# Pair 1 of a fused recurrence and MoE kernel loaded one token a row on GpSimd's queue, with a new instruction order

## The chip, the cores and the metric

The kernel runs on one core of one Trainium2 chip. A core has TensorE (matrix products, with a separate weight load), VectorE, ScalarE and GpSimd for the elementwise work, SyncE, which only issues transfers, and 16 DMA engines that all issuing engines share. The metric is the device time of one execution in microseconds (us); lower is better. Times within a profile count from the first instruction of the span. All engines run their own instructions strictly in order and wait for each other through semaphores.

## The reference

The kernel computes a gated linear recurrence over 768 tokens for 4 batches and 8 heads of 48 channels, and then feeds its output, as 3072 tokens of 384 channels, through two layers with a GELU between them.

```python
def _attn_ref(q, k, v, alpha):            # each (4, 8, 768, 48)
    state = zeros((B, H, D, D))
    for t in range(S):
        state = alpha[:, :, t, :, None] * state + einsum('bhd,bhe->bhde', k[:, :, t], v[:, :, t])
        y[:, :, t] = einsum('bhd,bhde->bhe', q[:, :, t], state)
    return y

def _moe_ref(x, w_in, w_out):             # x (3072, 384), w_in (384, 2048), w_out (2048, 384)
    h = x @ w_in
    g = 0.5 * h * (1.0 + tanh(sqrt(2 / pi) * (h + 0.044715 * h * h * h)))
    return g @ w_out
```

All inputs and the output are float32.

## The kernel before

**Tiling.** The 768 tokens of a batch are cut into 6 chunks of 128. One batch's chunk is a *unit* (128 tokens on the partitions, 8 heads x 48 channels along the row), two neighbouring batches' units make a *pair*, so there are 12 pairs, 0 to 11; pairs 0 and 1 are chunk 0. Within a chunk the recurrence is done as a masked attention with decay: `ln` takes the log of alpha (ScalarE), `cum` sums it over the tokens with an upper triangular matrix (TensorE), `b`, `binv` and `bend` are exponentials of the sums (ScalarE), `qp` = q*b and `kp` = k*binv (VectorE), `t` turns both so that channels lie on the partitions (TensorE) and `ev` copies them out of PSUM, `attn` multiplies them, `mask` keeps the lower triangle (VectorE), `y` multiplies the masked products with v, `x` copies y to bf16, `tx` turns it and `xe` copies it to `xT`. `kv` and `st` carry the state on to the next chunk. From pair 2 on the state's part of y is computed beside the attention. From pair 6 on the turns of q, k and x are transposing DMAs on SyncE's queue (`turn`).

**The two layers.** Layer 1 (`l1`, L658) makes the hidden tiles of a pair: each task is 6 products of 128 x 256 columns into one PSUM bank, and eight tasks make a pair's block; task `l1m.i` needs quarter i//2 of w_in, `xT` of both units, and one of the four PSUM buffers `ff`. `gelu` (ScalarE) empties it. Layer 2 (`l2`, L677) makes a unit's output in four tasks of four products of 384 columns, each needing one quarter of w_out; `ot` copies it out and `store` writes it.

**Two ways of laying out a pair.** Pairs 0 and 1 are `PACKED` (L179): q, k and alpha come with four tokens of a head in one row (768 bytes in one piece, L341), which needs a special sum (`cum_packed`, L375: 7 products with two block triangular matrices and 4 small ones for the last row), rearranging copies, and a turn back of k (`turn_back`, L511, and its copy L523) before `kv`. Their units are handled one at a time (`SINGLE`, `EARLY`). Pairs 2 and up come with one token a row (192 bytes a piece, one head each). Pairs 2 to 5 are turned as row tiles (`turn_halves`, L474: 32 products of 64 x 64 that go two at a time, copies in two halves, L491), and the last row of the sums is taken by VectorE's 32 x 32 transposes (`last_row`, L586) instead of by `bend`. `SPLIT` pairs are loaded and summed a unit at a time.

**Transfers.** `RINGS` lists the loads on the hardware queues: q, k and alpha of pairs 0 and 1 by unit, twelve loads of 192 KB; numbers in `BY_ACT` are issued by ScalarE, the rest by SyncE. `LOADS` lists what GpSimd's queue issues, in order; a `gate` is a small GpSimd copy that reads a tile and so holds that queue until the tile has landed. v of the `NARROW` pairs 0 and 1 is loaded as float32 and cast by VectorE or ScalarE (`narrow`, L423); all other v are cast by the DMA. The weights are cast by the DMA too.

**The order.** `Scheduler` (L47 to L165) builds the order of all instructions. `FIRST` (L184) is a list written out of every step, `E:task` with E one of P (TensorE), V (VectorE), A (ScalarE), G (GpSimd) and S (SyncE); `order()` puts the tasks in that order. Only the order of the steps of one engine matters for the chip: what is emitted is each engine's queue, and the waits between engines. `fill.n` steps are n idle products on TensorE (L322). `LANDED` holds landing times in nanoseconds that the scheduler assumes for the loads named; the numbers count the loads as they are declared, first those of `RINGS`, then those of `LOADS`.

PSUM has 8 banks: one double buffer `ca` of two banks, two `yk` and four `ff`. `CUM_FF` pairs keep their sums in `ff`, `AT_FF` names the units whose attention products go to `ff`.

The head of the old `FIRST`, by engine, is: SyncE alpha, alpha, q, k of pair 0 and then pair 1's; ScalarE q and k of unit 0 of pair 0; GpSimd gate on pair 0's second alpha, v of pair 0, gate on its second k, w_in 0, v of pair 1, w_in 1, 2, 3, w_out 0, 1, the first halves of pair 2. TensorE has `fill.7`, the packed sums of both units, and then ten more idle products in seven places between the steps of pairs 0 and 1.

Of the kernel before, what the change touches and what calls it, by code (L numbers as in the profile page):

```python
# [7 lines left out]
F32 = mybir.dt.float32  # L8
# [163 lines left out]
class _Kernel:  # L172

    BLOCKS = ((0,), (1,), (2,), (3,), (4,), (5,), (6,), (7,), (8,), (9,), (10,), (11,))
    SPLIT = (2,)
    EARLY = (0, 1)
    LOADS = ('gatea 0 1', 'v0', 'gatek 0 1', 'in 0', 'v1', 'in 1', 'in 2', 'in 3', 'out 0', 'out 1', '2a', 'out 2', '2b', 'out 3', '3', '4', '5', 'win3', '6', '7', '8', '9', '10', '11')

    PACKED, CUM_FF, R = (0, 1), (0, 1), 4  # L179
    RINGS = (('a', 0, 0, 1), ('a', 0, 1, 2), ('q', 0, 0, 1), ('k', 0, 0, 1), ('q', 0, 1, 2), ('k', 0, 1, 2),  # L180
             ('a', 1, 0, 1), ('a', 1, 1, 2), ('q', 1, 0, 1), ('k', 1, 0, 1), ('q', 1, 1, 2), ('k', 1, 1, 2))
    BY_ACT = (2, 3,)

    FIRST = """  # L184
        A:table.0 A:load.2 A:load.3 S:load.0 S:load.1 S:load.4 A:ln0.0 S:load.5 P:fill.7 P:cum0.0 A:ln0.1 G:gate.0 G:load.12 S:load.6 P:cum0.1 A:b0.0
        S:load.7 A:bend0.0 V:qp0.0 A:binv0.0 A:binv0.1 S:load.8 V:kp0.0 P:fill.2 P:t0.0 A:b0.1 V:ev0.0 P:fill.1 P:t0.1 S:load.9 A:ev0.1 V:qp0.1
        S:load.10 A:bend0.1 P:fill.3 P:attn0.0 V:kp0.1 G:gate.1 S:load.11 P:t0.2 G:load.13 V:mask0.0 A:ev0.2 P:t0.3 G:load.14 V:mask0.1 A:ev0.3
        P:fill.1 P:t0.4 V:ev0.4 P:fill.1 P:attn0.1 A:ln1.0 G:load.15 P:t0.5 V:mask0.3 P:cum1.0 A:ev0.5 G:load.16 V:vb0.0 A:ln1.1 P:y0.0 V:mask0.2
        G:load.17 P:kv0.0 A:binv1.0 P:cum1.1 V:st0.0 A:x0.0 G:load.18 A:vb0.1 V:kp1.0 P:tx0.0 A:b1.0 P:y0.1 V:xe0.0 G:load.19 V:qp1.0 P:t1.1 A:x0.1
        A:bend1.0 G:load.20 A:b1.1 P:fill.1 P:t1.0 A:ev1.0 V:ev1.1 G:load.21 V:qp1.1 P:fill.1 P:kv0.1 V:st0.1 G:load.22 A:binv1.1 A:bend1.1 P:tx0.1  # L190
        P:attn1.0 V:xe0.1 G:load.23 G:load.24 G:load.25 G:load.26 P:t1.2 P:l10.0 V:kp1.1 V:mask1.0 V:mask1.1 G:load.27 G:load.28 P:t1.3 A:ev1.2
# [513 lines left out]
    def tasks(self):  # L705
# [59 lines left out]
        for m, (c, i) in enumerate(pairs):  # L765
# [40 lines left out]
            if m in self.SPLIT:  # L806
                cums[1].deps += exps[:2]
# [228 lines left out]
```

## Time and profile before

| what | us |
|---|---|
| median of 3 runs (173.99 to 174.16) | 174.1 |
| the profiled execution | 173.77 |
| its span, first to last instruction | 171.9 |
| TensorE busy | 166.3 |
| layer 1 products (L658, 576) | 69.4 |
| layer 2 products (L677, 416) | 68.9 |
| attention products (L552, 192) | 8.0 |
| idle products (L327, 17) | 6.5 |
| ScalarE busy | 125.5 |
| VectorE busy | 107.7 |
| GpSimd busy | 63.0 |

A busy time counts a product from its issue to its modelled end, and products overlap in the pipeline, so a group's busy time is more than the time that the queue spends on it: six products of layer 1 are 0.65 us of the queue. "Idle before" in the waits is time in which an engine had nothing running, with what ended it. The DMA queues moved 29.4 MB, 17.7 of them on GpSimd's queue. The column PEclk of the page is the clock that the throttle granted; it reads 1.00 in every window.

### The profile page before, as it was taken

To read this page: it belongs to the slowest core of one execution; us is meant where nothing else is said; L and a number is where in the kernel's file an instruction comes from. 1 tells how busy PE (TensorE), PEld (TensorE's weight loads), DVE (VectorE), ACT (ScalarE), POOL (GpSimd) and SP (SyncE) were. 2 spreads that over 40 slices of the span, in tenths; PEclk is the share of its full clock that TensorE was granted. 3 is DMA by queue.
4 is the path that set the end of the run, shared out by engine and by line. 5 is a ranking of instruction groups with operands and counts; after the bars stand their busy time and mean duration, and the time that the engine had idled before them with its cause. 6 is when DMAs were issued, how large, how long until landed. Compare 5 with 4: busy or idle time off the path is not lost.

```text
span 171.9 us, 4595 instructions
## 1 busy us (share of the span) xinstructions
PE 166.3 (97%) x1909; PEld 129.8 (75%) x1909; DVE 107.7 (63%) x210; ACT 125.5 (73%) x205; POOL 63.0 (37%) x88
## 2 busy tenths in 40 slices
PE   7999999999999999999999999999999999999991
PEld 2566899666886896797697797796797978987860
DVE  6499820588978999998892898865947550100100
ACT  4578889897999798899779499868882636651412
POOL 2396546986504674933565435320000000000000
PEclk9999999999999999999999999999999999999999
DMA  4999999999999999999999999897967504001212
GB/s 138 311 268 217 199 247 230 231 230 228 256 208 96 257 218 241 169 165 242 145 224 213 158 226 138 181 233 60 232 186 148 147 1 114 4 0 40 101 48 92
DMA packets 51541, 29.40 MB, mean 171 GB/s; under 512 B 39616, under 2 KB 47936, under 8 KB 51520
## 3 DMA queue, kind: packets, MB, share of 16 engines
q0 software_dynamic: 26464, 17.70, 62.3%
q1 hardware_dynamic: 24512, 11.01, 30.8%
q10 hardware_dynamic: 544, 0.39, 0.8%
q8 instruction: 15, 0.25, 0.6%
q14 instruction: 6, 0.05, 0.1%
HBM read 25.17 MB, written 4.72 MB: 174 GB/s over the span
## 4 chain that ended last, share of the span: by engine, by line
PE 91%; DMA 3%; ACT 3%; DVE 0%; issue 0%; DVEq 0%
PE hT L658 37%; PE acc L677 37%; PE at L552 4%; DMA k<-in_k_dram 3%; PE yps L627 2%; PE cum L416 2%; PE kv L581 2%; PE qkT_ps L484 1%; PE xT_ps L646 1%; PE qkT_ps L470 1%; PE yps L561 1%; ACT qkT L508 1%; PE k_ps L516 1%; ACT L318 1%; PE idle L327 1%; PE yps L617 1%
## 5 line engine op out<-in xcount | busy, mean ns | idle before, releaser
L658 PE MATMUL hT<-xT,w_in 128*128 128x256 bf16 x576 | 69.4, 273 | 0.0
L677 PE MATMUL acc<-w_out,gT 128*128 128x384 bf16 (+3 forms) x416 | 68.9, 314 | 0.0
L664 ACT ACTIVATE gT<-hT 128x512 bf16<-128x512 f32 x96 | 53.6, 600 | 15.2 <-PE hT L658 13.1
L658 PEld LDWEIGHTS <-w_in 128*128 128x128 bf16 x576 | 60.6, 114 | 1.2 <-DMA w_in<-in_moe_w_in_dram 0.3
L677 PEld LDWEIGHTS <-gT 128*128 128x128 bf16 x416 | 37.4, 98 | 20.2
L571 DVE TENSOR_TENSOR atm<-at,ut 128x512 bf16<-128x512 f32 x48 | 30.1, 683 | 8.2 <-PE at L552 8.0
L689 DVE COPY ot<-acc 128x384 f32<-128x384 f32 (+2 forms) x9 | 4.3, 488 | 20.0 <-PE acc L677 20.0
L689 ACT COPY ot<-acc 128x384 f32<-128x384 f32 (+1 forms) x17 | 7.9, 472 | 11.6 <-PE acc L677 9.3
L595 DVE STREAM_TRANSPOSE tr<-b 32x256 f32<-32x256 f32 x32 | 14.0, 438 | 1.4 <-ACT b L449 0.8
L346 POOL DMA_DIRECT2D k<-in_k_dram x11 | 12.2, 1111 | 5.7 <-DMA v<-in_v_dram 1.7
L346 POOL DMA_DIRECT2D a<-in_alpha_dram x11 | 12.3, 1117 | 4.4 <-issue 1.7
L460 DVE TENSOR_TENSOR qp<-q,b 128x768 bf16<-128x768 f32 (+1 forms) x15 | 11.9, 792 | 2.8 <-ACT b L449 2.6
L346 POOL DMA_DIRECT2D vb<-in_v_dram x11 | 12.2, 1105 | 3.6 <-issue 1.9
L346 POOL DMA_DIRECT2D q<-in_q_dram x11 | 12.2, 1112 | 2.5 <-DMA w_out<-in_moe_w_out_dram 1.0
L449 ACT ACTIVATE binv<-cum 128x768 bf16<-128x768 f32 (+1 forms) x15 | 10.1, 684 | 3.3 <-PE cum L416 3.3
L460 DVE TENSOR_TENSOR kp<-k,binv 128x768 bf16<-128x768 f32 (+1 forms) x15 | 11.9, 791 | 0.5 <-ACT binv L449 0.5
L318 ACT ACT_TABLE_LOAD x9 | 11.5, 1283 | 0.9 <-PEq L1020 0.7
L449 ACT ACTIVATE b<-cum 128x768 f32<-128x768 f32 (+1 forms) x15 | 10.3, 685 | 2.0 <-PE cum L416 1.5
L664 ACT ACT_TABLE_LOAD x9 | 11.5, 1283 | 0.2
L606 DVE TENSOR_TENSOR stmp<-kv,st 128x384 f32<-128x384 f32 x16 | 8.9, 555 | 1.9 <-PE kv L581 1.2
L608 DVE TENSOR_TENSOR st<-stmp,tr 128x384 bf16<-128x384 f32 x16 | 8.9, 558 | 0.6
L399 ACT ACTIVATE la<-a 128x768 f16<-128x768 f32 (+1 forms) x11 | 8.5, 784 | 0.1
(74 smaller groups left out, 144.8 us busy)
## 6 DMA issues: line engine op xcount, KB each, us to landing
out_dram<-ot SPq DMA_DIRECT2D x19, 192.0 KB, 3.0
a<-in_alpha_dram POOLq DMA_DIRECT2D x9, 384.0 KB, 7.8
q<-in_q_dram POOLq DMA_DIRECT2D x9, 384.0 KB, 8.8
k<-in_k_dram POOLq DMA_DIRECT2D x9, 384.0 KB, 6.9
vb<-in_v_dram POOLq DMA_DIRECT2D x9, 192.0 KB, 6.3
w_in<-in_moe_w_in_dram POOLq DMA_DIRECT2D x4, 384.0 KB, 8.9
w_out<-in_moe_w_out_dram POOLq DMA_DIRECT2D x4, 384.0 KB, 11.0
out_dram<-ot SPq DMA_DIRECT2D x9, 96.0 KB, 1.9
```

Of the source, the lines that this page charges most:

```text
L318: nc.scalar.add_instruction(mybir.InstLoadActFuncSet(name=nc.get_next_instruction_name(), act_func_set_id=i, engine=mybir.EngineType.Activ ...
L346: dma(u[t][:, lo:hi].rearrange("t b h d -> t (b h) d"), src.rearrange("b h s d -> s (b h) d")[c * C:(c + 1) * C])
L449: self.nc.scalar.activation(u[n].rearrange("t i h d -> t i (h d)")[:, lo:hi], cum, AF.Exp, scale=1.0 if n == "b" else -1.0)
L460: self.nc.vector.tensor_tensor(out, rows, b, op=ALU.mult)
L571: self.nc.vector.tensor_tensor(u["atm", i][:, o], u["at", i][o], self.ut[:, None, :].to_broadcast([self.C, self.H // 2, self.C]), op=ALU.mult)
L595: self.nc.vector.transpose(u["tr"][f:f + 32, :, 0:32], rows[:, lo:lo + H * 2 * D].rearrange("t (g n) -> t g n", n=2 * D)[:, :, 0:32])
L606: nc.vector.tensor_tensor(s, acc, old, op=ALU.add)
L608: nc.vector.tensor_tensor(new, acc, end[:, :, None].to_broadcast([C, H // 2, 2 * D]), op=ALU.mult)
L658: self.nc.tensor.matmul(h[:, s].rearrange("p (g t) -> p g t", t=self.C), w_in[:, j, nt % 4 + s], self.xT[c % self.NX][:, lo:hi, j], start= ...
L664: return lambda e: self.nc.scalar.activation(self.gT[c % self.NG][:, nt:nt + 2, lo * self.C:hi * self.C], f.pop(("h", c, lo, nt)), AF.Gelu ...
L677: self.nc.tensor.matmul(f["acc", c, b][:, lo:hi], self.gT[c % self.NG][:, nt, b * self.C:(b + 1) * self.C], self.w_out[:, nt, lo:hi], star ...
L689: self.copy(e)(f["ot", c, b][:, sl], f["acc", c, b] if half is None else f["acc", c, b, half][:, sl])
```

## The change

The changed kernel treats pair 1 like pair 2 (split, one token a row, row tiles, last row by VectorE), but without a state. Its q, k and alpha leave the hardware queues and become half loads on GpSimd's queue, between w_in 0 and w_in 1. v of pairs 0 and 1 is cast by the DMA, v of pair 1 in two halves. GpSimd's first gate is on the first alpha instead of the second, and the gate on k is gone. ScalarE issues one load instead of two. Pair 1's sums stay in `ff`, now one bank for each unit. Four of pair 0's layer-1 tasks (`APART`) are split by unit: `h1` does unit 0, `l1` unit 1 of the same bank. Layer 2 no longer names all layer-1 tasks of pairs 0 and 1 as a dependency. `FIRST` is new from the first step to the last; it keeps `fill.7` and has no other idle products.

```diff
-    SPLIT = (2,)
-    EARLY = (0, 1)
-    LOADS = ('gatea 0 1', 'v0', 'gatek 0 1', 'in 0', 'v1', 'in 1', 'in 2', 'in 3', 'out 0', 'out 1', '2a', 'out 2', '2b', 'out 3', '3', '4', '5', 'win3', '6', '7', '8', '9', '10', '11')
+    SPLIT = (1, 2)
+    EARLY = (0,)
+    LOADS = ('gatea 0 0', 'v0', 'in 0', 'a1', 'q1', 'k1', 'in 1', 'v1', 'in 2', 'in 3', 'out 0', 'out 1', '2a', 'out 2', '2b', 'out 3', '3', '4', '5', 'win3', '6', '7', '8', '9', '10', '11')
-    PACKED, CUM_FF, R = (0, 1), (0, 1), 4
-    RINGS = (('a', 0, 0, 1), ('a', 0, 1, 2), ('q', 0, 0, 1), ('k', 0, 0, 1), ('q', 0, 1, 2), ('k', 0, 1, 2),
-             ('a', 1, 0, 1), ('a', 1, 1, 2), ('q', 1, 0, 1), ('k', 1, 0, 1), ('q', 1, 1, 2), ('k', 1, 1, 2))
-    BY_ACT = (2, 3,)
+    PACKED, CUM_FF, R = (0,), (0, 1), 4
+    RINGS = (('a', 0, 0, 1), ('a', 0, 1, 2), ('q', 0, 0, 1), ('k', 0, 0, 1), ('k', 0, 1, 2), ('q', 0, 1, 2))
+    BY_ACT = (2,)
     FIRST = """
-        A:table.0 A:load.2 A:load.3 S:load.0 S:load.1 S:load.4 A:ln0.0 S:load.5 P:fill.7 P:cum0.0 A:ln0.1 G:gate.0 G:load.12 S:load.6 P:cum0.1 A:b0.0
-        S:load.7 A:bend0.0 V:qp0.0 A:binv0.0 A:binv0.1 S:load.8 V:kp0.0 P:fill.2 P:t0.0 A:b0.1 V:ev0.0 P:fill.1 P:t0.1 S:load.9 A:ev0.1 V:qp0.1
-        S:load.10 A:bend0.1 P:fill.3 P:attn0.0 V:kp0.1 G:gate.1 S:load.11 P:t0.2 G:load.13 V:mask0.0 A:ev0.2 P:t0.3 G:load.14 V:mask0.1 A:ev0.3
+        S:load.0 S:load.3 A:table.0 A:load.2 G:gate.0 G:load.6 G:load.7 G:load.8 G:load.9 G:load.10 G:load.11 S:load.4 G:load.12 G:load.13 G:load.14
+        G:load.15 S:load.1 A:ln0.0 G:load.16 G:load.17 S:load.5 P:fill.7 A:ln0.1 P:cum0.0 A:binv0.0 P:cum0.1 V:kp0.0 P:t0.1 A:b0.0 A:b0.1 A:binv0.1
+        A:ev0.1 V:qp0.0 V:qp0.1 V:kp0.1 P:t0.0 P:t0.2 V:ev0.2 A:ev0.0 A:bend0.0 A:bend0.1 P:t0.3 P:attn0.0 A:ev0.3 V:mask0.0 V:mask0.1 P:t0.4 A:ev0.4
+        P:t0.5 P:attn0.1 A:ev0.5 G:load.18 G:load.19 G:load.20 G:load.21 G:load.22 G:load.23 P:kv0.0 G:load.24 G:load.25 G:load.26 G:load.27 G:load.28
+        G:load.29 G:load.30 G:load.31 G:load.32 G:load.33 A:ln1.0 P:y0.0 V:st0.0 G:load.34 V:mask0.2 V:mask0.3 P:cum1.0 A:x0.0 P:tx0.0 V:xe0.0 P:kv0.1
+        A:ln1.1 P:cum1.1 V:st0.1 A:b1.0 A:binv1.0 A:b1.1 P:y0.1 A:x0.1 P:tx0.1 V:qp1.0 V:qp1.1 A:binv1.1 V:kp1.0 P:h10.0 V:xe0.1 P:h10.1 P:l10.0
+        V:kp1.1 P:t1.0 A:gelu0.0 A:ev1.0 P:l10.1 V:tr1.0 V:ev1.1 V:tr1.1 V:tr1.2 A:gelu0.1 P:h10.2 P:l10.2 P:attn1.0 V:mask1.0 P:h10.3 V:mask1.2
+        P:l10.3 V:mask1.3 A:gelu0.2 P:l10.4 P:l10.5 A:gelu0.4 A:gelu0.3 P:y1.1 V:mask1.1 P:y1.0 A:x1.0 V:x1.1 P:l10.7 P:tx1.1 V:tr1.3 V:xe1.1 P:tx1.0
+        P:l10.6 V:xe1.0 P:kv1.1 P:l11.0 A:gelu0.7 A:gelu0.5 V:st1.1 A:gelu0.6 P:l11.7 P:l11.3 P:l11.1 A:gelu1.0 A:gelu1.7 A:gelu1.3 P:l11.5 A:gelu1.1
+        P:l11.4 A:gelu1.5 A:gelu1.4 G:load.35 P:l11.2 A:gelu1.2 P:l11.6 P:l20.0 P:l20.3 P:kv1.0 P:l20.7 A:ln2.0 A:ln2.1 P:cum2.0 G:load.36 A:binv2.0
+        V:st1.0 P:l20.4 A:b2.0 V:qp2.0 G:load.37 G:load.38 G:load.39 G:load.40 G:load.41 G:load.42 G:gate.1 P:l20.11 P:cum2.1 A:b2.1 V:kp2.0 A:binv2.1
...
-    LANDED = {"load.0": 2800, "load.1": 3400, "load.2": 4400, "load.3": 5000, "load.4": 6000, "load.5": 7300, "load.12": 10100, "load.6": 9200, "load.7":
...
+    LANDED = {"load.0": 3780, "load.1": 4880, "load.2": 4330, "load.3": 5430, "load.4": 5979, "load.5": 6570, "load.6": 8629, "load.7": 10530,
...
-    NARROW = (0, 1)
+    NARROW = ()
+    APART = (0, 2, 4, 6)
-    LAST_ROW = (2, 3, 4, 5, 6, 7, 8, 9)
+    LAST_ROW = (1, 2, 3, 4, 5, 6, 7, 8, 9)
-    AT_FF, SINGLE = {0: (1,), 1: ()}, (0, 1)
+    AT_FF, SINGLE = {0: (1,)}, (0,)
...
-                nc.tensor.matmul(cum[:, i, 0:H * D], self.ut_h, la[:, i, :, 0:D], start=True, stop=True)
+                rows = cum[lo] if u["apart"] else cum[:, i]
+                nc.tensor.matmul(rows[:, 0:H * D], self.ut_h, la[:, i, :, 0:D], start=True, stop=True)
...
-    def layer1(self, f, c, lo, hi, nt):
+    def layer1(self, f, c, lo, hi, nt, units=None):
+        a, b = units or (lo, hi)
+
         def emit(e):
             w_in = self.w_in[nt // 4].rearrange("k j (c r) -> k j r c", r=self.NFT // 4)
-            h = f["h", c, lo, nt] = self.tile("ff", [self.C, 2, (hi - lo) * self.C], F32, "hT")
+            if a == lo:
+                f["h", c, lo, nt] = self.tile("ff", [self.C, 2, (hi - lo) * self.C], F32, "hT")
+            h = f["h", c, lo, nt]
             for s in range(2):
                 for j in range(self.NKT):
-                    self.nc.tensor.matmul(h[:, s].rearrange("p (g t) -> p g t", t=self.C), w_in[:, j, nt % 4 + s],
-                                          self.xT[c % self.NX][:, lo:hi, j],
+                    self.nc.tensor.matmul(h[:, s, (a - lo) * self.C:(b - lo) * self.C].rearrange("p (g t) -> p g t", t=self.C), w_in[:, j, nt % 4 + s],
+                                          self.xT[c % self.NX][:, a:b, j],
                                           start=j == 0, stop=j == self.NKT - 1, skip_group_check=True)
...
-                t = s.add("l1", {"PE": W["l1_4"]}, 10000 + n, self.layer1(f, c, lo, hi, nt),
-                          [xts[c, b] for b in range(lo, hi)] + [loads["w", "in", nt // 4]], stream=n - 16 if m > 1 else None)
+                h1 = []
+                if m == 0 and nt in self.APART:
+                    h1 = [s.add("h1", {"PE": W["l1_2"]}, 10000 + n, self.layer1(f, c, lo, hi, nt, (lo, lo + 1)), [xts[c, lo], loads["w", "in", nt // 4]])]
+                t = s.add("l1", {"PE": W["l1_2" if h1 else "l1_4"]}, 10000 + n, self.layer1(f, c, lo, hi, nt, (lo + 1, hi) if h1 else None),
+                          [xts[c, b] for b in range(lo, hi)] + [loads["w", "in", nt // 4]] + h1, stream=n - 16 if m > 1 else None)
...
-                t = s.add("l2", {"PE": W["l2"]}, 10000 + n, self.layer2(f, c, b, part),
-                          gs[m if m else b // 2][2 * part:2 * part + 2] + [loads["w", "out", min(part, 3)]] + firsts, stream=n - 16)
+                t = s.add("l2", {"PE": W["l2"]}, 10000 + n, self.layer2(f, c, b, part),
+                          gs[m if m else b // 2][2 * part:2 * part + 2] + [loads["w", "out", min(part, 3)]], stream=n - 16)
```

In the new numbering loads 0 to 5 are alpha, alpha, q, k of the first unit and k, q of the second, all of pair 0; 6 is v of pair 0, 7 is w_in 0, 8 to 13 are the halves of alpha, q, k of pair 1, 14 is w_in 1, 15 and 16 are v of pair 1, 17 and 18 w_in 2 and 3, 19 and 20 w_out 0 and 1. SyncE's queue thus starts with loads 0, 3, 4, 1, 5: alpha and k of the first unit, then k, alpha and q of the second.

More of the change, by code (lines that the diff above doesn't have):

```diff
@@ L437, in emit @@
                 out = u[n][:, lo:hi]
-                if u["packed"]:
+                if u["apart"]:
                     self.nc.scalar.activation(out[:, 0], u["cum"][lo][:, H * D:H * D + H // 2], AF.Exp)
@@ L801, in tasks @@
             if m in self.CUM_FF:
-                cums[0].take("ff", *exps[:3])
-                cums[1].take("ff", *exps[3:])
+                cums[0].take("ff", *exps[:len(exps) // 2])
+                cums[1].take("ff", *exps[len(exps) // 2:])
             else:
                 cums[0].take("ca", *exps)
-            if m in self.SPLIT:
+            if m in self.SPLIT and m not in self.CUM_FF:
                 cums[1].deps += exps[:2]
```

102 lines of the change are left out of this document (46 added, 56 removed), and 9 rows, old and new, of the table LANDED.

## The prediction

> **What bounds the kernel now.** I read the page first, then the chain of waits, the timeline of the first 48 us, and last the DMA view cut into narrow windows, which gives each transfer's time to landing. From the page:
>
> ```profile
> span 171.9 us, 4595 instructions
> ...
> PE 166.3 (97%) x1909; PEld 129.8 (75%) x1909; DVE 107.7 (63%) x210; ACT 125.5 (73%) x205; POOL 63.0 (37%) x88
> ...
> PE 91%; DMA 3%; ACT 3%; DVE 0%; issue 0%; DVEq 0%
> ```
>
> TensorE is the bound. The chain says from when:
>
> ```profile
> 1.92 5.28 DMA k<-in_k_dram
> ...
> 15.33 0.59 ACT qkT L508
> 15.92 0.04 issue
> 15.96 0.33 PE xT_ps L646 x3
> 16.29 0.33 PE at L552 x8
> ...
> 20.69 0.85 PE hT L658 x6
> ...
> 22.61 0.17 PE xT_ps L646 x3
> 22.78 0.66 PE hT L658 x6
> ...
> 29.51 1.95 PE acc L677 x12
> ...
> 163.12 5.21 PE acc L677 x32
> ...
> 168.36 0.48 ACT ot L689
> ```
>
> Up to 16.3 the chain goes through loads, ScalarE copies and idle products; from there every piece but one of 0.03 us is TensorE's, until 168.36. What follows (copy, store, end) is 3.5 us and the change leaves it alone. So a gain can only come from reaching the same point of the TensorE queue earlier, and any hole made after 16.3 adds in full.
>
> The second thing to see is what paces TensorE between 17 and 23. The tiles of pair 0's layer 1 need the four parts of w_in in turn. By the DMA view the parts land at 14.34, 18.75, 20.64 and 22.55; the last line below is the last of them, issued at 11.93 and 10.6 us on its way (the line above it is the k for which the chain waits in its first piece). The first tile of part 2 starts at 20.69, that of part 3 at 22.78.
>
> ```profile
> 1.19 3.17 PE L327 MATMUL idle<-zero 128*128 128x512 bf16 x7 [1.19 <-DVE ones L990]
> ...
> 8.14 0.81 PE L327 MATMUL idle<-zero 128*128 128x512 bf16 x3
> ```
> ```profile
> k<-in_k_dram ACTq DMA_DIRECT2D x1, 192.0 KB, 5.3
> ```
> ```profile
> w_in<-in_moe_w_in_dram POOLq DMA_DIRECT2D x1, 384.0 KB, 10.6
> ```
>
> The idle products start 0.42 us apart at first and 0.216 us apart at 8.1: TensorE begins at half pace and speeds up near 5.6 (there the packed sums' products halve too). The page's clock row shows full speed throughout, so only these spacings tell.
>
> **TensorE work removed.** By the chain's pieces: pair 1's packed sums, 2 x 0.76 us, become two products of 384 columns, 0.165 each (layer 2 does four such in 0.65): -1.19. Its four turns of 0.22 become one of 0.57 by row tiles (L484): -0.31. Turning k back, 2 x 0.22: -0.44. Together -1.94. Ten idle products of 0.216: -2.16, of filler. Splitting four layer-1 tiles by unit makes 48 products of 128 columns from 24 of 256; 128-column products run 0.055 apart (0.22 for four turns), 12 x 0.055 = 0.66, the same as 0.655 before: nothing. None of this moves the end by itself: it counts only if layer 1 gets its data earlier.
>
> **When the data come.** Removed from the hardware queues: pair 1's six loads, which land 0.51 to 0.58 apart. GpSimd's first gate now waits for the first alpha (landing 3.77) and not the second (4.79); gone is the gate on k (its wait ended at 8.05). So v of pair 0 is issued at 3.95 instead of 4.96 and the first w_in right behind it, at 5.2 instead of 8.52. GpSimd's first packets flowed 2.5 us after the first issue, so 6.5 now. Then by intervals between landings in the old queue: v with a cast 1.2 (pair 5's, 1.21), w_in 1.9 each, half loads of one token a row 0.76 (pair 2's a, q, k: 0.86, 0.85, 0.59, 0.94, 0.78, 0.58), half v 0.5. Receipt 0.5. Landings: v0 8.2, w_in 0 10.1, pair 1's a, q, k to 14.7, w_in 1 16.6, v1 17.6, w_in 2 19.5, w_in 3 21.4. GpSimd gets six issues of 0.9 more, and SP is rid of them; issue keeps ahead all the same: 1.25 + 0.75 + 6 x 0.9 us puts the last of pair 1 out at 11.4, 3 us before it lands. From w_in 1 on each issue waits for the landing of the eighth transfer before it (w_in 1 for v0, w_in 2 for the second alpha half, 11.6), all past by then. Bounds: packed in without gaps (6 x 0.51 + 1.2 + 4 x 1.9 + 6 x 0.76 + 2 x 0.5 = 17.5 us of transfer from 2.2 on) w_in 3 lands at 20.2; with the dearest half (0.94) as price for all six, at 22.5. I take 21.7, a little late of the middle, and 19.8 for w_in 2, since the old queue lost 2.5 us against its own sum (12 x 0.51 + 2 x 1.8 + 4 x 1.9 from 2.2 would have been 20.0, and was 22.55).
>
> **The new startup, step by step.** SP now issues a, k, k, a, q of pair 0, so the second alpha is SP's fourth load, issued at 2.85. It lands not before 5.75 (issue plus the 2.9 of the early loads) nor after 7.4 (the fifth landing of before was 7.41); nearest is the byte count: five loads are 0.98 MB, the window of the first 5 us moves 0.755 (151 GB/s), the next 309 GB/s, so 5.75, and 0.5 to 0.7 of receipt: 6.45. Behind it on ScalarE waits the second ln, and behind that, in order, both binv and b, hence all of pair 0's scaling. With ScalarE steps of 0.39 to 0.48, VectorE 0.47 (scaling) and 0.605 (mask, turn copies): ln 6.5; binv 6.9; second sums on TensorE 7.0 to 7.8; kp 7.4 to 7.9; last b 8.3; the second kp ends 9.4; first attention 9.8 to 10.1; its masks to 11.5; second attention 11.1; y of unit 0 11.6 (v, cast on its way, is there since 8.2; before it landed at 11.06 and its cast ended at 12.3); its x 12.3; masks of unit 1 to 13.3; y of unit 1 13.5. The x of unit 1 queues on ScalarE behind pair 1's ln and three exps (alpha landed 11.6): 13.9 to 14.4. Then its turn, and layer 1 starts with unit 0 at 14.6, both units at 15.74. Pair 1's kp ends 16.2, its turn 16.8, its attention 18.3, layer 1 of w_in 1 is done at 19.0. Then w_in 2 is awaited until 19.8: a hole of 0.8, which hides up to 0.6 us more delay of the startup (0.6 and not 0.8, since pair 1's masks run to 20.9 and its second y would be the next to be late). The last w_in lands at 21.7: its first tile at 21.73, against 22.78.
>
> From there both kernels have the same queue, except that unit 0's x of pair 1 (0.17) is still to be turned, and that pair 1's layer 1 waits 0.39 for that copy (VectorE has xT of the other unit before it). Left after 22.78 before: 168.36 - 22.78 = 145.58. So the end of TensorE: 21.73 + 145.58 + 0.17 + 0.39 = 167.87, or **-0.49**. The kv of unit 1, now before l20 instead of behind it, only changes place. w_out and pair 2 land about 0.9 earlier in the same order: hidden behind the 7 us of layer 1 that follow. VectorE loses three casts of v and two copies and gains a turn copy and four transposes of 0.27; ScalarE loses three turn copies, a cast and two small exps, about 2 us; what of this lies on the startup's path is in the steps above, the rest lies beside layer 1.
>
> **The rest of the order.** From 30 us on the order is new throughout. Where I laid it beside the old one, the work between an attention and its y, between sums and turn, and from SP's transposes to their use is of the same size (transposes landed 2.7 to 8.4 us after issue; SP's queue gives each 2 us or more of margin). Tightest: pair 3's first y stands 1.3 us behind its attention where two masks need 1.4, against 2.28; pair 2's turn 1.95 behind its sums, against 2.12. I price the holes at 0 to 0.5 and, since gains are excluded there (there is no hole to close), take 0.1 within rounding.
>
> The profiled run was 173.77, 0.33 under the median of 174.1. So 174.1 - 0.5 = **173.6**. Its own range: w_in 3 at 21.2 (the second y's limit 21.15) to 22.3: 173.1 to 174.2.
>
> **Rivals.** *TensorE slows down again (slower).* The ten idle products go; in 5.6-9.0, 9.0-12.4 and 12.4-15.8 TensorE then works 1.3, 1.9 and 1.7 us by the steps above, 38 to 56%, where the old timeline's pieces, idle products counted, never fall under 69%. If half pace returns and lasts into layer 1, 3.4 us at half pace lose 1.7, the startup's own products 0.7; less the 0.6 hidden: -0.5 + 1.8 = +1.3, 175.4. It decides once a stretch under some 50% is enough. For it: half pace at the start of the run. Against: the longest gap I find is 1.2 us (5.8 to 7.0). The Trainium skill ("TensorE: Matmul & The Clock Gate", "Part 1: The HAM clock gate (the "warmup" mystery)") says that the array falls back after an idle window of about 3.4 us; by that rule there is no such gap here and the sum stands. Its passage on a second failure mode tells of short idle times between groups that also make the clock swing, which would be this rival; no stretch of this trace shows either.
>
> *Small packets hold the queue (slower).* Pair 1's packets shrink from 768 to 192 bytes and stand ahead of w_in 1 to 3. If each half costs 0.94, w_in 3 lands near 22.75, 6 x 0.18 later than in the sum: +1.1 on -0.5, or 174.7. For it: the two 0.86 and 0.94 above; against: the 0.59 and 0.58 beside them.
>
> *More.* The queue runs without gaps, w_in 3 at 20.2: then the masks bind at 21.15 and the wait for the copy may vanish: -1.1 to -1.5, 172.8.
>
> *A wash.* The second alpha at 7.4 (0.95 late, 0.37 past the cover) or holes of 0.4 to 0.5 behind 30 us: 174.0 to 174.1. The change would then only move TensorE's idle time from filler to waiting.
>
> **Chances.** Forecast 0.42; slowing down 0.18; small packets 0.20; more 0.10; wash 0.10. A run can be told from no change beyond about 0.2%, 0.35 us. Faster (under 173.75): 0.26 of the forecast's, all of more, and 0.05 of the rest: 0.41. Same: 0.13 of the forecast's and 0.06 of the wash: 0.19. Slower 0.40. The range, 172.7 to 175.4, leaves out the tail of each end.
>
> **What would show it.** Right: w_in 3's first product near 21.7; idle products only up to 4.4; the second ln of ScalarE near 6.5 after a wait for alpha; a TensorE wait for w_in 2 near 19 to 20. Wrong: 256-column products of layer 1 at 0.22 apart (slowing down); w_in 3 landing after 22.5 (small packets); TensorE idle for over 0.5 us anywhere past 30.

## The result, and the profile after

| what | before | after |
|---|---|---|
| median of 4 runs, us | 174.13 (173.99 to 179.07) | 181.32 (179.66 to 182.93) |
| ratio, 95% interval | | 1.038 (1.029 to 1.048) |
| the profiled execution, us | 173.77 | 182.93 |
| its span, us | 171.9 | 181.0 |
| TensorE idle in it behind its first product, gaps over 0.15 us | 0.5 | 10.8 |
| last part of w_in landed at | 22.55 | 24.37 |
| TensorE's last product ended at | 168.3 | 177.6 |

The change makes the kernel slower; 173.6 had been forecast. One thing is needed to read the times below: single executions of every kernel here, the one before included (12 of 57, up to 187.2), now and then take 2.5 us or more longer than the fastest of the same kernel, and the ratios leave these out where they stand out. In a second comparison (e17 below) the changed kernel's ratio is 1.017 (1.011 to 1.022) and its fastest execution 175.28; beside that, all four of the first are long. So there are two losses to explain: some 2 to 3 us that are always there, and a larger one that comes in part of the executions.

The page of the changed kernel, its span, busy times, clock row and shares of the chain:

```profile
span 181.0 us, 4581 instructions
...
PE 165.4 (91%) x1911; PEld 129.7 (72%) x1911; DVE 109.4 (60%) x210; ACT 124.2 (69%) x199; POOL 68.0 (38%) x94
...
PEclk9858999999999999999999999999969999999999
...
PE 65%; DMA 27%; POOL 2%; DVE 1%; issue 1%; ACT 1%; SPq 1%; ACTq 0%
```

TensorE is busy for 0.9 us less than before, and the span is 9.1 longer: most of it is waiting, and some of it half pace (the 8 and 5 in the first quarter of the clock row, the 6 at 131 to 136 us). The chain that ended last is no longer TensorE's alone; 27% of it is transfers. Which ones is told by its pieces (start, length, what):

```profile
5.22 7.34 DMA w_in<-in_moe_w_in_dram
...
15.53 8.83 DMA w_in<-in_moe_w_in_dram
...
76.17 14.35 DMA qkT<-kp
```

and by the list of TensorE's waits (total us, times, longest):

```profile
PE at L554 <- DMA qkT<-kp: 2.5, 1, 2.5
PE cum L385 <- ACT la L398: 2.2, 1, 2.2
PE hT L664 <- ACT ot L695: 2.2, 1, 2.2
...
PE hT L664 <- DMA w_in<-in_moe_w_in_dram: 0.9, 1, 0.9
PE cum L418 <- ACT la L400: 0.9, 1, 0.9
```

Three places, in order of time. *The start*: the second packed sums wait 2.2 us for the second alpha (landed 6.91), layer 1's third part waits until 22.48 for its weights, and the fourth part, whose loading is the second piece above, lands at 15.53 + 8.83 = 24.4. The attention of pair 2 starts at 39.61, against 37.42: 2.2 late. *The middle*: pair 6's turned k takes 14.35 us, where before it took 7.4, and its attention waits 2.5 for it; a load of alpha beside it costs another 0.9. Pair 6's attention stands 5.5 late, of which 3.3 is new. *Near 129 us*: a layer-1 bank waits 2.2 us for an output copy, which waited for a buffer of `ot` that a store (125.11 to 130.53) still held. Behind that the clock falls for a window. The same by stretches (length, TensorE busy, granted clock, share of the DMA engines, GB/s):

```profile
4.46:7.87 3.41, 1.19 (x15) 1.00 1.28 203
...
7.87:11.28 3.41, 2.85 (x30) 0.50 1.30 183
11.28:14.70 3.42, 3.33 (x39) 0.50 1.06 242
...
127.30:130.70 3.40, 1.57 (x38) 1.00 1.42 210
130.75:134.16 3.41, 3.08 (x15) 0.50 1.14 232
```

TensorE worked for 1.19 and 1.57 of 3.4 us in the two windows ahead of the slow ones; 3.41 us at half pace lose 1.7, and 5.5 + 2.2 + 1.7 = 9.4, against the 9.2 by which its last product is late (177.55 for 168.32).

### The profile page after: what moved, and what is told of

It reads as the page before. It is cut to its first block, busy times and chain, and to the rows that moved or that the text cites. A ratio compares the mean times of both kernels' runs of the same rounds, so it can differ in the third digit from the quotient of the medians.

```text
span 181.0 us, 4581 instructions
## 1 busy us (share of the span) xinstructions
PE 165.4 (91%) x1911; PEld 129.7 (72%) x1911; DVE 109.4 (60%) x210; ACT 124.2 (69%) x199; POOL 68.0 (38%) x94
## 4 chain that ended last, share of the span: by engine, by line
PE 65%; DMA 27%; POOL 2%; DVE 1%; issue 1%; ACT 1%; SPq 1%; ACTq 0%
PE acc L683 28%; PE hT L664 27%; DMA w_in<-in_moe_w_in_dram 9%; DMA qkT<-kp 8%; DMA a<-in_alpha_dram 7%; DMA out_dram<-ot 3%; PE at L554 3%; PE yps L629 2%; POOL vb L347 2%; PE cum L418 1%; PE qkT_ps L486 1%; PE kv L583 1%; PE yps L563 1%; SPq L536 1%; PE xT_ps L648 1%
## 5 line engine op out<-in xcount | busy, mean ns | idle before, releaser
L664 PE MATMUL hT<-xT,w_in 128*128 128x256 bf16 (+1 forms) x600 | 70.8, 272 | 3.3 <-ACT ot L695 2.2
L670 ACT ACTIVATE gT<-hT 128x512 bf16<-128x512 f32 x96 | 54.5, 600 | 18.4 <-PE hT L664 16.1
L664 PEld LDWEIGHTS <-w_in 128*128 128x128 bf16 x600 | 62.0, 114 | 5.6 <-DMA xT<-x 1.6
L597 DVE STREAM_TRANSPOSE tr<-b 32x256 f32<-32x256 f32 x36 | 15.7, 437 | 2.0 <-ACT b L451 1.1
L347 POOL DMA_DIRECT2D vb<-in_v_dram x14 | 15.3, 1094 | 3.7 <-issue 1.7
L347 POOL DMA_DIRECT2D k<-in_k_dram x13 | 14.1, 1084 | 4.4 <-DMA w_out<-in_moe_w_out_dram 2.1
L347 POOL DMA_DIRECT2D q<-in_q_dram x13 | 14.1, 1085 | 3.9 <-DMA w_out<-in_moe_w_out_dram 1.0
L347 POOL DMA_DIRECT2D a<-in_alpha_dram x13 | 14.1, 1085 | 3.8 <-DMA w_in<-in_moe_w_in_dram 1.3
L462 DVE TENSOR_TENSOR kp<-k,binv 128x768 bf16<-128x768 f32 (+1 forms) x15 | 11.9, 793 | 4.0 <-ACT binv L451 3.6
L451 ACT ACTIVATE binv<-cum 128x768 bf16<-128x768 f32 (+1 forms) x15 | 10.2, 679 | 4.2 <-PE cum L418 3.5
L639 DVE CAST x<-yps 128x384 bf16<-128x384 f32 x10 | 5.5, 556 | 11.9 <-PE yps L629 8.6
L451 ACT ACTIVATE b<-cum 128x768 f32<-128x768 f32 (+1 forms) x15 | 10.2, 681 | 3.1 <-ACT la L400 2.1
L400 ACT ACTIVATE la<-a 128x768 f16<-128x768 f32 (+1 forms) x13 | 9.6, 744 | 1.7 <-DMA a<-in_alpha_dram 1.6
```

Of the source, the lines that this page charges most:

```text
L347: dma(u[t][:, lo:hi].rearrange("t b h d -> t (b h) d"), src.rearrange("b h s d -> s (b h) d")[c * C:(c + 1) * C])
L400: self.nc.scalar.activation(u["la"][:, lo:hi, :, 0:self.D], u["a"][:, lo:hi], AF.Ln)
L451: self.nc.scalar.activation(u[n].rearrange("t i h d -> t i (h d)")[:, lo:hi], cum, AF.Exp, scale=1.0 if n == "b" else -1.0)
L462: self.nc.vector.tensor_tensor(out, rows, b, op=ALU.mult)
L597: self.nc.vector.transpose(u["tr"][f:f + 32, :, 0:32], rows[:, lo:lo + H * 2 * D].rearrange("t (g n) -> t g n", n=2 * D)[:, :, 0:32])
L664: self.nc.tensor.matmul(h[:, s, (a - lo) * self.C:(b - lo) * self.C].rearrange("p (g t) -> p g t", t=self.C), w_in[:, j, nt % 4 + s], self ...
```

## The experiments

**e1, e2: which part of the order.** Every engine's order is a list, so the new start and the old rest can be joined, and the other way round.

```diff
 FIRST (e1): the changed list up to P:l20.0, then
-  the changed list from P:l20.0 on
+  the list of before from P:l20.0 on (loads and gates renumbered)
 FIRST (e2): the list of before up to P:l20.0, then the changed list
```

> The changed kernel up to the first product of layer 2 of chunk 0, the order of the kernel before on every engine from there on. Holes theory (the loss is made in three places: the start 2.2 us by late weights, the wait at pair 6's turned rows some 3.4, the hole near 129 us and the slow clock behind it some 3.9): only the start's loss is left, 176.3 us, attention of pair 2 near 39.6 as in the changed kernel, no TensorE gap over 0.5 us after 40 us. Rival, the start alone sets all later collisions of loads, turned rows and stores: the holes come back, 179 to 181 us. Rival, the start's loss is made good behind it: 174 to 175 us.

> The kernel before up to the first product of layer 2 of chunk 0, the changed kernel's order on every engine from there on. Holes theory: 174.1 + 5 = 179 us, with a TensorE gap of 2 us or more at pair 6's attention and another near 127 us with a slow clock window after it. Rival, the late start sets the collisions: no gap over 0.5 us, 174.1 to 174.5 us. In between (one of the two holes): 176 to 178 us, and the profile says which one.

e1: 176.12, 176.19, 176.24 and 177.07; ratio 1.012 (1.006 to 1.017). The start's loss and nothing else, as expected. TensorE's waits over 0.2 us are all in the first 17 us:

```profile
PE cum L384 <- ACT la L397: 1.7, 1, 1.7
PE idle L327 <- DVE ones L996: 1.2, 1, 1.2
PE yps L618 <- DVE xT L651: 0.6, 1, 0.6
PE xT_ps L647 <- DVE qp L461: 0.6, 1, 0.6
PE qkT_ps L471 <- ACT qkT L509: 0.6, 1, 0.6
```

e2: 175.1, 178.26, 178.76 and 181.37, with the wait for pair 6's k (2.0 us) in the profiled one and no gap near 127 us. So the later loss comes with the new order behind the start and doesn't need the late start, and it doesn't come in every execution. Of the kernel before, measured beside these, three of seven were long too, so that this rests on the wait in the profile more than on the times.

**e3, e4: idle products back in the changed kernel; the gate away.**

```diff
 e3:  P:cum0.0
+     P:fill.8       (and P:fill.3 behind t0.0, P:fill.1 behind t0.3)
 e4: -LOADS = ('gatea 0 0', 'v0', 'in 0', ...
     +LOADS = ('v0', 'in 0', ...
```

> The changed kernel with 12 idle products more in the start (8 between the two packed sums, 3 behind the turns of unit 0, 1 behind those of unit 1), so that TensorE has no idle window in the first 15 us. Theory that late weights hold the start: the clock shows no half window from 7.9 to 14.7, the work up to 15 us is done 0.5 to 1 us sooner, and part 2 of layer 1 still starts at 22.5 with its weights; the time stays within 0.5 of the changed kernel's 181.3. Rival, the slow clock in the start costs what the start lost: 2 us less, 179.3 us.

> The changed kernel without the wait of GpSimd's first load for the first alpha: v of pair 0 is issued near 1.9 in place of 3.95, w_in right behind it, and so on. Theory that GpSimd's queue can't move its first loads while the six direct loads share the rings: v lands 1 us earlier at most, the third part of w_in at 21.5 or later, the first alphas land 0.5 to 1.5 later; time 180.3 to 182. Rival, a fixed 6 us from GpSimd's first issue to its landing: v lands near 8, the third part of w_in near 20.4, part 2 of layer 1 starts 2 us earlier, and the time is 179.3 us.

e3 gave 176.37, 183.17, 184.56 and 186.27; the profiled one of these waits 4.6 us for pair 6's k. The start is as the first theory said in its main point: part 2 of layer 1 still waits for its weights (22.77), though TensorE ran at full pace to 16.3; a slow window remained behind that. The total says nothing, because the middle's loss lies over it.

e4 settles one thing. v of pair 0 was issued at 1.76 in place of 3.95 and landed at 10.30 in place of 10.11; the third part of w_in landed at 22.20 in place of 22.48. Issuing 2.2 us sooner bought 0.3 at most. What it cost is in the chain:

```profile
2.85 6.76 DMA a<-in_alpha_dram
```

The second alpha landed at 9.61 and TensorE stood still from 5.5 to 10.2. Times: 177.63 to 183.82. The loads delay each other: those issued sooner on GpSimd's queue hardly landed sooner, and the direct loads beside them landed up to 3.2 us later (q of the second unit at 10.68 in place of 7.45).

**e5 to e8: the start on the quiet base (e1), one cause at a time.**

```diff
 e5: -NARROW = ()
     +NARROW = (0, 1)       (v of pairs 0, 1 as float, casts on V and A)
 e6: +P:fill.8 P:fill.3 P:fill.1 P:fill.2 P:fill.2   (five places before l10.0)
 e7: e5 and e6
 e8: e7, and
     -S:load.0 S:load.3 S:load.4 S:load.1 S:load.5
     +S:load.0 S:load.1 S:load.3 S:load.4 S:load.5
```

> The kernel of the new start and the old rest (176.2 us), with v of pairs 0 and 1 loaded as floats and narrowed by VectorE and ScalarE, as before the change. Theory that the cast on the way costs the rings: the 2048 packets of 96 bytes of a pair (29 ns each, 3.7 us of the 16 engines) become some 90 packets of 3.5 to 4.2 KB (220 ns, 1.3 us), so v of pair 0 lands near 8 in place of 9.55 and the third and fourth parts of w_in at 19 to 20.5 and 21 to 22.4 in place of 22.51 and 24.39. TensorE, slowed from 17 to 20.4, is then the later one: 175 to 175.6 us. Rival, pair 1's rows of 192 bytes hold the queue alone: the fourth part stays at 24 or later, 176.2 us.

> The kernel of the new start and the old rest (176.2 us) with 16 idle products more in the start (8 between the packed sums, 3 and 1 behind the turns of units 0 and 1, 2 and 2 around y of unit 1). Theory of two causes that cover each other: the clock window at half pace (16.97 to 20.38) goes or moves, TensorE comes sooner to part 2 of layer 1 and waits there for its weights until 22.5: 175.9 to 176.4 us. Rival, the clock alone: 174.5 to 175 us.

> Both of these edits in one kernel. Two causes that cover each other: with the weights at 19 to 20.5 and TensorE at full pace the start's loss is gone, 174.0 to 174.7 us, and part 2 of layer 1 starts at 20.5 to 21.2. Rival, one cause alone: no better than the better of the two single edits.

> The kernel with both edits, and SyncE issues the second alpha of pair 0 as its second load in place of its fourth, as before the change. The second alpha lands near 4.8 in place of 6.9 and the second packed sums start 1.5 to 2 us sooner; the k of unit 0 lands near 7. If the weights are what TensorE waits for: within 0.3 of the kernel with both edits; if the second alpha still sets the start: 0.5 to 1.2 us less, 173.2 to 173.8.

| kernel | executions, us | part 3 of w_in landed | part 4 |
|---|---|---|---|
| e1 | 176.12 176.19 176.24 177.07 | 22.51 | 24.39 |
| e5 float v | 176.25 176.90 176.94 178.60 | 22.17 | 24.20 |
| e6 idle products | 175.78 176.38 177.51 184.62 | 22.53 | 24.43 |
| e7 both | 175.60 175.68 175.85 178.55 | 22.32 | 24.21 |
| e8 both, alpha second | 175.93 176.84 178.20 183.12 | 21.80 | 24.24 |

My theory of the cast fell: v as float lands no sooner than v cast on the way, though its packets are fewer. Idle products give back some: in the profiled executions the fourth part's first product starts 0.4 us sooner in e6 than in e1, and 1.1 sooner in e7 than in e5. By the ratios to the kernel before beside each (1.012 in e1; 1.019, 1.018, 1.011 and 1.018 in e5 to e8, another comparison) none of them is shown to be faster than e1. In e7 the granted clock is 1.00 in every stretch of the start, and TensorE, now early enough, waits for weights twice:

```profile
PE hT L664 <- DMA w_in<-in_moe_w_in_dram: 1.4, 2, 0.8
```

The alpha's place adds nothing on top (e8). In all five kernels the fourth part lands at 24.2 to 24.4, and 14 of the 20 executions take 175.6 to 177.1. In the other kernels with the changed kernel's loads (e3, e4, e9 to e11, e16 to e18) it lands at 24.1 to 25.2. What holds the start is when the weights land, and none of these edits moves the fourth part by more than 0.2 us.

**e12, e13: queue or rows.** Pair 1's half loads with one token a row (192 bytes) go back to SyncE (e12, on e1's base); or the kernel before, with its packed rows (768 bytes), hands pair 1's six loads to GpSimd behind the first part of w_in (e13).

```diff
 e12: RINGS   +('a',1,0,1) ('a',1,1,2) ('q',1,0,1) ('q',1,1,2) ('k',1,0,1) ('k',1,1,2)
      LOADS   -'a1', 'q1', 'k1'
 e13: FIRST   -S:load.6 ... S:load.11
              +G:load.6 ... G:load.11     (behind G:load.13)
```

> The kernel of the new start and the old rest (176.2 us), with pair 1's six half loads of one token a row issued by SyncE, behind pair 0's, as before the change, in place of GpSimd. It tells the queue from the packets. If 192-byte rows cost 0.8 us a half wherever they are issued: they land 0.8 apart to 12.5 or later and the fourth part of w_in at 24 or later, 176 to 177 us. If it is GpSimd's queue that moves them slowly: they land 0.5 apart by 10.5 to 11, the fourth part of w_in lands at 22.5, and the time is 174.7 to 175.5 us (the clock's slow window stays).

> The kernel before, with pair 1's six packed loads (768-byte rows) issued by GpSimd behind the first part of w_in, in place of SyncE. If the rows of 192 bytes are what costs: these land 0.5 to 0.55 apart, the fourth part of w_in at 22.3 to 23, the time 174.0 to 174.6 us. If it is GpSimd's queue that moves 200 KB in 0.8 us whatever the rows: 0.8 apart, the fourth part at 24 or later, 175.3 to 176.2 us.

e12 met neither: 191.81 to 195.65, and the last half of k landed at 33.1, 18 us after its issue. Layer 1 waited for it:

```profile
PE hT L664 <- DVE xT L652: 11.6, 1, 11.6
```

Rows of 192 bytes on SyncE's queue lose against the big packets of GpSimd's: where both are in flight, SyncE's halves land 2 to 10 us apart. So of the two queues GpSimd's is the better one for this layout; there its rows are put together in packets of up to 4.2 KB.

e13: 178.35 to 181.43; the fourth part landed at 26.40, outside both expectations. Two things are mixed in it. The six packed halves landed in 3.72 us (12.88 to 16.60, 0.5 to 0.66 apart from the third on), against 4.88 (12.56 to 17.44, 0.81 apart) for the rows of 192 bytes on the same queue. The DMA view shows it as a rate, for two us in which hardly anything else was on the way; the changed kernel from 12.7 to 14.7, then e13 from 13.2 to 15.2:

```profile
DMA packets 154, 0.43 MB, mean 213 GB/s; under 512 B 35, under 2 KB 55, under 8 KB 154
```
```profile
DMA packets 240, 0.74 MB, mean 370 GB/s; under 512 B 59, under 2 KB 59, under 8 KB 240
```

Both put rows together in packets of some 4 KB; one of 22 rows of 192 bytes took 0.32 us, one of 6 rows of 768 bytes 0.18. So the same queue can move the packed loads at 0.5 each, and the rows are worth 1.2 to 1.9 us over six halves, where the weights are 1.8 late. But in e13 the first part of w_in was issued only behind its gate, at 8.18, the DMA engines stood almost idle near 10 us, v of pair 1 (as float) landed 3.1 behind the last half, and the later parts of w_in came 1.9 to 2.7 apart; that ate more than the rows saved. That the rows are what makes the weights late is therefore likely and not shown.

The Trainium skill ("DMA: Bandwidth & Descriptors", "Specifications") states 512 bytes as the least transfer for full rate. The two stretches agree in direction, 213 against 370 GB/s.

**e14, e15: two parts of the change alone, in the kernel before.** v of pairs 0 and 1 cast by its load (e14); the ten later idle products out (e15; its expectation says twelve).

```diff
 e14: -NARROW = (0, 1)          e15: -P:fill.2 P:fill.1 P:fill.3 P:fill.1
      +NARROW = ()                   -P:fill.1 P:fill.1 P:fill.1
      -V:vb0.0 A:vb0.1 V:vb1.0 V:vb1.1
```

> The kernel before, with v of pairs 0 and 1 cast by its load and the four casts on VectorE and ScalarE left out: this part of the change alone. As the float loads of e5 landed no sooner than the cast ones, the fourth part of w_in stays within 0.4 of 22.55 and the time within 0.4 of 174.1. Rival, the 96-byte packets hold the queue: 24 us, 175.5.

> The kernel before without its later idle products (12 products of 0.216 us; the first seven stay): this part of the change alone. Theory from e6 and e7, that the clock falls back for a window in the start: one or two windows at half pace between 8 and 19 us, 174.3 to 175.5 us. Rival, no window: 173.8 to 174.2.

e14: ratio 1.000 (0.996 to 1.005); its part 4 landed at 22.23. e15: 173.28, 174.54, 178.54 and 181.47; in the profiled one, the first of these, part 4 landed at 21.80, the clock stayed at full pace through gaps of 0.4 to 0.7 us, and TensorE ended at 167.78, 0.5 sooner than before. Neither part is seen to cost anything by itself.

**e9 to e11, e16 to e18: the middle.** How far must the new order go for the loss to appear? And is it the one step that I suspected: in the changed order VectorE scales pair 6's k ahead of the masks of pair 5, so that SyncE issues the second transpose of pair 6 some 3.2 us behind the first, where it was 5.3.

```diff
 e9:  changed list up to P:l14.0, list of before from there on
 e10: changed list up to P:l25.0, list of before from there on
 e11: changed list, with          e16: the same step in e10's list
 -V:ev5.1 V:kp6.0 V:tr6.1
 +V:mask5.3 V:kp6.0
 e17: the changed kernel          e18: e1's list, with
                                  -V:mask5.3 ... V:kp6.0
                                  +V:ev5.0 V:kp6.0
```

> The changed kernel's order on every engine up to the first product of layer 1 of pair 4, the order of before from there on, so that pair 6's turned rows, the stores and the loads around them are issued as before the change. Theory that the new order around pair 6's turned rows costs the 3 to 5 us: 176 to 177 us in most runs, no TensorE gap over 1 us at pair 6's attention. Rival, the loads' order between 30 and 65 us sets it: 179 us or more in most runs, with the gap.

> The changed kernel's order up to the first product of layer 2 of pair 5, thus with the new order around pair 6's turned rows, the order of before behind it. Theory: the gap at pair 6's attention is back in most runs (2 us or more, and 1.7 where the clock then drops for a window), 178 to 181 us. Rival, the loss is made behind 95 us: 176 to 177 us in most runs.

> The changed kernel with one step moved on VectorE: the scaling of pair 6's k behind the masks of pair 5, as before the change, which lets SyncE issue the second turned load of pair 6 some 2 us or more later (5.3 us behind the first in place of 3.2). Theory that the two transposes one behind the other are what holds the loads: the second lands within 8 us of its issue, the gap at pair 6's attention is under 0.5 us, and the median falls from 181.3 to 177 to 178. Rival, the slow stretch comes whatever the distance of the two: the second lands later still, gap 2 us or more, 181 us or more.

> The changed kernel's order up to the first product of layer 2 of pair 5 and the old order behind it (180.4 us median, four of six executions at 179.5 or more), with the scaling of pair 6's k moved behind the masks of pair 5. If the distance of the two transposes is the cause: at least five of six executions at 176 to 177.5. If not: half of them or more at 179 or above.

> The changed kernel once more, unchanged, beside e18 on one chip. If the loss in the middle belongs to its order: at least four of six executions at 179 or above, as the four before. If it was the chip: most at 176 to 177.5.

> The new start with the old order behind it (176.2 us, all four executions within 1 us), with the scaling of pair 6's k moved ahead on VectorE, in front of the masks of pair 5, as in the changed kernel, so that the second transpose follows the first by some 3 us in place of 5.3. If that distance is the cause: half of the executions or more at 178.5 or above, with a gap of TensorE at pair 6's attention in a profile of such a one. If not: five of six at 176 to 177.2.

| kernel | second transpose behind the first | executions, us |
|---|---|---|
| e9 new to 14 | late (5.8) | 175.83 176.71 176.72 176.85 177.88 178.99 |
| e10 new to 25 | early (3.2) | 175.99 176.79 179.49 181.28 183.34 186.93 |
| e11 changed, k later | late (6.7) | 175.93 176.72 177.06 177.60 183.38 183.52 |
| e16 e10, k later | late (6.7) | 176.19 177.35 177.62 177.65 177.84 180.02 |
| e17 changed | early (3.2) | 175.28 176.20 176.86 177.08 177.34 181.41 183.10 |
| e18 e1, k earlier | early (2.5) | 176.01 176.12 177.20 180.66 182.44 183.49 |

e9 to e11 and, elsewhere, e16 show the loss where the second transpose follows early, and mostly not where it follows late; e16's five shorter executions, 176.19 to 177.84, lie a little above what it expected. e17 went against its first expectation, two of seven and not four of six, and nearer to its second, that the first four were the chip's: five of seven take 175.3 to 177.3. What made those four long is not shown. e18's three of six meet the first of its two. Counted over all kernels, with an execution called long that is 2.5 us or more above the fastest of its kernel (the changed kernel's eleven taken as one set): 21 of 35 with the step early (the changed kernel 6 of 11; e2, e3, e4, e10, e18), 14 of 56 with it late (e12 left out), and 12 of 57 in the runs of the kernel before beside them. By these counts the share of long executions is three in five with the step early, and one in four with it late; but most of these kernels differ in more than the step. In the three pairs that differ in it alone (the changed kernel and e11, e10 and e16, e18 and e1) it is 13 of 23 early (9 of 19 without the first four) and 3 of 16 late, no pair being measured in one comparison. The counts point to the step and don't prove it. Nor is the wait bound to it: the profiled executions of e5 and e13, with the step late, wait 1.6 and 2.0 us for pair 6's k.

What happens in a long one is seen in the DMA view of 76 to 82 us. The kernel before, then the changed one, then e18:

```profile
DMA packets 1031, 1.32 MB, mean 221 GB/s; under 512 B 665, under 2 KB 793, under 8 KB 1030
...
k<-in_k_dram POOLq DMA_DIRECT2D x1, 384.0 KB, 6.9
...
qkT<-kp SPq DMA_TRANSPOSE x1, 7.4
```
```profile
DMA packets 1011, 0.56 MB, mean 94 GB/s; under 512 B 919, under 2 KB 938, under 8 KB 1010
...
k<-in_k_dram POOLq DMA_DIRECT2D x1, 384.0 KB, 13.3
qkT<-kp SPq DMA_TRANSPOSE x1, 14.4
```
```profile
DMA packets 1157, 0.64 MB, mean 107 GB/s; under 512 B 1066, under 2 KB 1068, under 8 KB 1156
...
k<-in_k_dram POOLq DMA_DIRECT2D x1, 384.0 KB, 14.6
qkT<-kp SPq DMA_TRANSPOSE x1, 15.8
```

The transposes move 256-byte packets, the loads packets of 4.2 KB. In the changed kernel's stretch a 4.2 KB packet took 0.76 to 1.15 us (means over 2 us), where the kernel before has 0.23 to 0.33; everything issued from 72.8 us on, the loads, a store and both transposes, then takes 11 to 15 us. Slow packets of the loads are not the whole of it: in e18's stretch they took 0.23 to 0.34, and yet hardly more was moved. The same slowing shows in good executions too, but for some 2 us (e1: 0.87 us a packet at 76 to 78, 0.37 at 78 to 80). Why it lasts 6 us in one execution and 2 in the next isn't shown, nor whether something outside the kernel sets it off; the long executions of the kernel before left no profile.

The third place is less bound to the order: e16's long execution has it with the old order behind 95 us, and so has e18's. In e16:

```profile
PE hT L664 <- ACT ot L695: 2.3, 1, 2.3
```

In the four profiles that show it (the changed kernel's two, e16, e18) the store that held the buffer took 4.4 to 5.7 us; in e1 and before the stores there took 2.1 to 2.2. I did not vary that step alone.

## Why the prediction was wrong

**What bounds the kernel: right.** From the last part of w_in on, the order's length is fixed. My sum behind the fourth part's first product was 145.58 + 0.17 + 0.39 = 146.1. In e1, e6 and e7, which have the old order behind the start and no later gap, that product starts at 24.84, 24.48 and 24.25 and TensorE ends at 170.90, 170.56 and 170.65: 146.1, 146.1 and 146.4.

**When the data come: this step failed.** It gave 8.2, 10.1, 14.7, 16.6, 19.8 and 21.7 for v, the first part of w_in, pair 1's k, and the other three parts; they landed at 10.11, 12.56, 17.44, 19.12, 22.48 and 24.37. The fourth part is 2.7 late, and outside the bounds (20.2 to 22.5). Put in the sum, 24.4 + 146.1 = 170.5 for TensorE's end, 2.2 behind the old one: that is e1, and the steady part of the loss. Three terms were mis-sized, and they make up 1.9, 0.55 and 0.3 of the 2.7.

The largest is the time from GpSimd's first packets to the landing of v: the sum had 1.2 and 0.5 of receipt for it. The first packets flowed as forecast, or sooner (at 5.99, for "so 6.5 now"), and v landed 4.1 us behind them. The old trace had 3.6 for the same way (7.47 to 11.06) and 6.1 from issue to landing of this v, then as float, against 6.2 now; I took the interval between two landings in a queue that is already flowing for the whole way of its first load. Neither the cast nor a late issue is the reason: with v as float it is 3.7 (e5, 6.19 to 9.86), with the issue 2.2 us sooner 5.8 (e4, 4.49 to 10.30). It is 2.5 in e13 (as float, 7.00 to 9.53), where nothing else was issued on that queue until 8.18; what else sets it is not shown. The receipt is not at fault: from the last packet to the landing the old trace has 0.3 us (k by ScalarE) to 0.8 (GpSimd's last load). The second term is the first part of w_in, 2.45 behind v where 1.9 was taken. The third is the price of a half load, 0.81 in place of 0.76, over six.

I had also noted that the old queue lost 2.5 us against its own sum, and allowed the new one almost nothing for it. The sum without gaps is 20.0 for the old loads and 20.2 for the new ones: with the same loss on top, the fourth part lands at 22.7, and no gain was to be had at the start.

**The startup's steps.** The second alpha landed at 6.91, inside 5.75 to 7.4 and 0.46 behind the value taken. Layer 1 began at 17.0, not 14.6: TensorE ran at half pace from 7.87 to 14.70 and the second alpha's lateness went through every step. I had covered only 0.6 of that by the wait for weights; as the weights came 2.7 late, they hid it: the fourth part's first product starts 0.04 us behind its landing in the changed kernel, and 0.04 behind in e17, where half pace lasted from 7.71 to 21.36. In e1, with the slow window at 16.97 to 20.38, 0.45 stayed uncovered, in e5 1.1.

**TensorE slows down again: this rival's mechanism came, its price did not.** I put the point of decision at under 50% of a window; the trace has 35% and 46% ahead of the two slow stretches. The share alone doesn't decide it: e1 has 60% (2.04 of 3.41 us, from 13.56 on) ahead of a slow window, and the changed kernel a window of 49% (1.69 of 3.41, from 86.37 on) with full pace behind it. And in the start it cost the changed kernel next to nothing, and e1 and e5 0.4 and 1.1 against e6 and e7, not 1.8, because the weights were later still. The Trainium skill ("TensorE: Matmul & The Clock Gate", "Part 1: The HAM clock gate (the "warmup" mystery)") has the array fall back after an idle window of some 3.4 us, and the windows are 3.41 long here; in these rows the window is not idle, only thinly used.

**Small packets hold the queue: nearest to what happened.** It gave 174.7 for w_in 3 at 22.75; the halves did cost 0.81 each, the lateness of v and of the first part of w_in came on top, and the kernels without a stall took 175.3 to 177.

**The rest of the order: this step failed too.** I priced the new order behind 30 us at 0 to 0.5, with "transposes landed 2.7 to 8.4 us after issue; SP's queue gives each 2 us or more of margin". The margin was there, and more: the second transpose of pair 6 was needed 11.9 us behind its issue. It took 14.35 in the profiled execution. I had measured margins against the durations of the old order, and did not ask what the new one does to the durations. The edit that the counts point to, a scaling moved ahead of four masks on VectorE, looked like a gain for SyncE's queue.

**TensorE work removed, and the casts: right that they count for nothing** (e14 1.000; e15's best execution within 0.1 of the best of before).

What stays open: why the slow stretch lasts 2 us in one execution and 6 in another, and why all of the first four were long; how much of the late weights is the order of the loads and not the rows; and whether e14 and e15 together, in the old kernel, gain anything, which was not tried. No version here was shown to beat the kernel before.

## What to carry to other kernels

Price a moved transfer by how long the same transfer took to land beside its neighbours, not by a sum of intervals between landings: here an earlier issue landed at most 0.3 us earlier (e4). A margin between a transfer's issue and its use holds only for the neighbours it was measured with; when the order around transposing loads changes, take their worst duration in the trace and double it (8.4 was the worst here, and up to 19.0 came, in e3). And run a kernel with transfers near their limit often enough to see its long executions: four agreed on 179.7 to 182.9 here, and seven more said 175.3 to 183.1.

## What was not expected of the hardware

- A transposing load and the large load beside it can both take twice as long: 14.35 us for the transpose and 13.3 for the load, 94 GB/s in all, against 7.4, 6.9 and 221 GB/s before. That they slow each other is likely and not shown. The Trainium skill ("Advanced Engine Details and Errata", "X-Bar Transpose (TRN2)") has transposing transfers as fast as plain ones; here they are about as fast as the plain ones beside them, and both are slow.
- Half loads of 192-byte rows on SyncE's queue, beside GpSimd's, took up to 19.7 us to land (e12); on GpSimd's queue, in the changed kernel and e1, 6.5 to 7.5.
- The clock fell after windows with TensorE 35%, 46% and, in e1, 60% busy, and stayed up after one with 49%. Once down it stayed so for two windows although TensorE was busy for 2.85 of the first one's 3.41 us; in e17 for four.
